# A linear-attention and expert kernel on Trainium2: five filling turnings become twelve small products, a decay table comes from two scans, and items 1 to 5 are ordered anew

## The chip, the cores and the metric

The kernel runs on one core of a Trainium2 chip. The metric is device time in microseconds (us), the median of several runs. The profile is one further execution, recorded by the hardware. A core has five engines that run their own instruction streams and wait for each other by semaphores: PE (TensorE, matrix products; each product is a weight load, shown as PEld, and a matmul), DVE (VectorE), ACT (ScalarE), POOL (GpSimd) and SP (SyncE, which here only issues DMAs).

## The reference

Two blocks follow each other. The first is a linear attention with a decay per channel (B=4 batches, H=8 heads, S=768 tokens, 48 channels per head), the second a layer of 8 experts (D=384, F=1024) with one expert per token; a gate lets a token keep the expert of the token before it.

```python
# attention, per batch and head
for t in range(S):
    kt, vt, rt = k[:, :, t], v[:, :, t], r[:, :, t]
    cur = einsum('bhd,bhe->bhde', u * kt, vt)
    y[:, :, t] = einsum('bhd,bhde->bhe', rt, state + cur)
    state = w * state + einsum('bhd,bhe->bhde', kt, vt)
x = y.transpose(0, 2, 1, 3).reshape(B, S, H * D_head)
# experts, per token
fresh_e = argmax(x @ w_gate)
e = fresh_e if s == 0 or sigmoid(x @ w_local) < 0.5 else prev_e
out[b, s] = softmax(x @ w_gate)[e] * (relu(x @ w1[e]) @ w2[e])
```

## The kernel before, in words

**Tiling.** The attention works on 16 items. Item n is one batch and one pair of heads (n // 4 and n % 4); a pair of heads lies on the partitions as two halves of 64. An item's 768 tokens are 6 chunks of 128. Within a chunk the sum over earlier tokens is a masked product of scores; across chunks the state is carried. Powers of the decay w, and their reciprocals, make both possible: rw is r times a power of w, kw is k times the reciprocal power.

**Steps of an item**, each with its method and the lines that the profile shows:

- load (L195 to L200): SP issues three transfers: rk, kv, vT. Up to four items are under way.
- scale (POOL): ke = k times the end powers (L214), pd = r times k (L218), rw (L235; items 0 to 2 have rw made by DVE in keys).
- keys (DVE): kw (L245), and for items 0 to 2 rw (L235).
- scores (L296, PE): 24 products in two halves, each into one of two PSUM banks called pair; DVE masks each half into am (L298).
- own (L275, PE): 4 products of pd with u, into the PSUM tile y; DVE multiplies y by vT (L281).
- added (L257, PE): 10 products of ke and v, the sums of each chunk, into a part of the PSUM tile mp.
- states (L263, DVE): one scan over these sums gives S, the state ahead of each chunk.
- inside (L305, PE): 12 products of am and v, added to y. before (L318, PE): 10 products of S and rw, added to y; ACT copies y out as xT (L326).
- turn (L337, PE): 6 transpositions of xT into a pair bank; ACT copies them to x (L339). logits (L349) and token_logits (L357) come once per batch and also use pair banks.

**Tables.** tab holds, for each of four head pairs, the powers 0 to 128 of w and of 1/w on each partition. They are made by doubling (L133): 7 multiplications, by DVE for pair 0 and by POOL for pairs 1 to 3. The powers of a pair are copied by ACT to first, a part of mp (L137, L383, L398). reciprocals refines the reciprocal powers in two steps on DVE (the newton steps, L157 and L158), from first into newton and inv. ends (ACT, L167 and L168) and turn_ends (PE, L174; ACT, L175) make the end powers, endT, on which ke depends; tables (ACT, L183) fills step, the factors of the scan S.

**What sets the order.** Every engine runs its instructions in the order in which they are issued, and that order is written out by hand in run (L363 on), with cases by item number; no scheduler changes it. Each call of banks takes the other one of the two pair banks, so a PE step that writes a pair bank waits until the reader of what stood there two calls ago is done. first, newton and the sums of added lie in the one tile mp. y has one buffer.

**Filling.** Ahead of item 0, PE has products that nothing uses: align(26) are 26 products of 32 by 32 by 128, warm(8) are 8 transpositions of 128 by 128, and, behind turn_ends for pair 0, warm(5) another 5.

Behind item 15 the expert stage follows: the router, hidden products, output products, gathers and scatters by DMA. It begins near 108 us and runs to the end.

Of the kernel before, what the change touches and what calls it, by code (L numbers as in the profile page):

```python
# [62 lines left out]
class Attention:  # L63
# [13 lines left out]
    def __init__(self, tc, st, rk_d, kv_d, vT_d, x_d, w_t, wp_d, kept, ident, lt, mp):  # L77
# [46 lines left out]
        w = once.tile([P, HP, 2], F32, name="w")  # L124
        nc.vector.tensor_scalar(w[:, :, 0], w_t[:, :, 0], W_LO, W_HI, Alu.max, Alu.min)
        nc.vector.reciprocal(w[:, :, 1], w[:, :, 0])
        nc.vector.tensor_copy(tab[:, 0, :, 1], w[:, 0])
        nc.gpsimd.tensor_copy(tab[:, 1:, :, 1], w[:, 1:])
        n = 2
        while n <= P:  # L130
            m = min(n - 1, P + 1 - n)
            for engine, t in ((nc.vector, tab[:, :1]), (nc.gpsimd, tab[:, 1:])):
                engine.tensor_mul(t[..., n:n + m], t[..., 1:1 + m], t[..., n - 1:n].to_broadcast([P, t.shape[1], 2, m]))  # L133
            n += m

        self.first, self.newton = mp[:, :P + 1], mp[:, P + 1:2 * P + 1]
# [6 lines left out]
        self.warm(8)  # L143
        self.ends(slice(0, 1))
        self.turn_ends(slice(0, 1))
        self.warm(5)

    def align(self, n):

# [211 lines left out]
    def run(self, router, fetch, heads):  # L361
# [11 lines left out]
        for n in range(M + 1):  # L373
            if n + AHEAD - 1 < M:
                self.load(n + AHEAD - 1)
            if n == 0:
                self.scale(0)
                self.keys(0)
                self.tables()
                self.scores(0, 0)()  # L380
                self.scores(0, 1)()
                self.own(0)
                self.nc.scalar.copy(self.first, self.tab[:, 1, 0])  # L383
                self.turn_ends(slice(1, HP))
                self.warm(3)
                self.added(0)
                self.reciprocals(1)
                self.states(0)
                self.scale(1)
                continue  # L390
            if n < 3:

                self.keys(n)
                self.inside(n - 1)
                self.before(n - 1)
                if n == 2:
                    self.turn(0, pair("tp"))
                self.nc.scalar.copy(self.first, self.tab[:, n + 1, 0])  # L398
                self.scores(n, 0)()
                keep = self.scores(n, 1)  # L400
                keep()
                self.own(n)
                self.added(n)
                self.states(n)
                if n == 1:
                    self.reciprocals(2)
                else:
                    router.numbering()
                self.scale(n + 1)
                continue  # L410
            if n < M:
                self.turn(n - 2, pair("tp"))
                if n == g + 7:
                    fetch(2)
                    router.head(self.inv[:, HP - 1])
                    heads()
                    self.own(n)
                if n == g + 6:
                    router.same(0, 1)
                if n == M - 2:  # L420
                    fetch(0)
                if n == 3:
                    self.reciprocals(3)
                if n < 5:
                    self.keys(n)
                if n > 3:
                    if n not in (g + 3, g + 5, g + 7):
                        self.added(n)
                    if n != g + 3:
                        self.states(n)  # L430
# [31 lines left out]
                continue  # L462

            ahead = n if n < 5 else n + 1
            if n == 3:
                self.added(3)
                self.states(3)
            if ahead < M:
                self.scores(ahead, 0)()
                if n == g + 6:  # L470
# [2 lines left out]
            if n % HP == 0:  # L473
# [7 lines left out]
                    router.ranks(0, (0,))  # L481
                self.logits(n // HP - 1, pair("lp")[0])
                if n == 4:
                    self.scores(5, 0)()
                    self.scores(5, 1)()
                    self.keys(6)
# [4 lines left out]
            else:  # L491
                if n == 3:
                    keep()
                self.own(n)
                if n == g + 2:
                    self.added(n + 1)
                    router.keys(0, mp)
# [1303 lines left out]
```

## Time and profile before

| what | value |
|---|---|
| time, median of 3 runs | 378.54 us (377.91 to 380.58) |
| the profiled execution's own time | 377.01 us |
| its span | 375.2 us |
| PE's mean granted clock | 0.997 of full speed |
| PE busy | 362.0 us (96%), 3844 instructions |
| PE weight loads | 318.4 us (85%) |
| DVE, POOL, ACT busy | 246.3, 152.1, 110.4 us |
| DMA | 74.93 MB, 200 GB/s in the mean |

In a row of the timeline stand the start in the span, the length, the engine, the line, the operation, out<-in, the size and the count (x24), and in brackets the idle time of the engine ahead of it with what ended it. Neighbouring instructions of a kind are one row; "issue" in brackets is a time in which the engine waited for nothing that the profile shows. The ends of matmuls are modelled. A group's row has the busy time and the mean of one in ns behind the first bar, and the idle time ahead of it behind the second.

### The profile page before, as it was taken

What the parts mean: (1) busy time and instruction counts of PE and PEld (TensorE: products, weight loads), DVE (VectorE), ACT (ScalarE), POOL (GpSimd) and SP (SyncE); (2) the same over time, 40 slices, a digit from 0 to 9 for tenths busy, and PEclk for the clock granted to TensorE, in tenths of its full rate; (3) what the DMA queues carried; (4) which work ended last, traced back from release to release, by engine and by line L of the source; (5) the groups of instructions that cost most, each with busy time, mean ns of one, the idle gap of its engine ahead of it and who ended that gap; (6) DMA issues with size and microseconds to landing.
All of it is one profiled execution on the core that took longest, in us unless ns stands there. A gap on an engine that the chain in (4) does not pass through costs nothing. (4 is left out here: it accounts for less than half of the span.)

```text
span 375.2 us, 9672 instructions
## 1 busy us (share of the span) xinstructions
PE 362.0 (96%) x3844; PEld 318.4 (85%) x3844; DVE 246.3 (66%) x717; ACT 110.4 (29%) x304; POOL 152.1 (41%) x212
## 2 busy tenths in 40 slices
PE   7899999999999999999999999999999999999992
PEld 6676777786769999989899999999998998989971
DVE  6988768788834845886567566857767767555300
ACT  4132232233432112322332233233233333331210
POOL 7689999789512055212433122313323023021012
PEclk9999999999999999999999999999999999999998
DMA  7999999983658749704342452264165064172011
GB/s 244 415 407 408 405 409 349 372 314 124 185 188 311 265 159 357 252 32 145 113 197 61 169 199 68 72 224 166 36 215 220 12 222 199 21 262 109 2 43 37
DMA packets 17765, 74.93 MB, mean 200 GB/s; under 512 B 2778, under 2 KB 6624, under 8 KB 15408
## 3 DMA queue, kind: packets, MB, share of 16 engines
q1 hardware_dynamic: 10336, 56.89, 41.1%
q0 software_dynamic: 3424, 9.48, 7.4%
q10 hardware_dynamic: 3952, 7.87, 5.7%
q8 instruction: 32, 0.52, 0.6%
q14 instruction: 21, 0.17, 0.1%
HBM read 64.79 MB, written 9.47 MB: 198 GB/s over the span
## 5 line engine op out<-in xcount | busy, mean ns | idle before, releaser
L1353 POOL DMA_INDIRECT out_dram<-yo,sid x27 | 26.6, 984 | 115.5 <-ACT yo L1348 92.0
L1204 PE MATMUL h<-exT,w1t 128*128 128x168 f32 (+4 forms) x240 | 54.9, 327 | 0.0
L1208 DVE TENSOR_TENSOR hT<-h,hs 128x168 f32<-128x168 f32 (+3 forms) x60 | 21.1, 351 | 46.2 <-PE h L1204 29.6
L1127 POOL DMA_INDIRECT xg<-x_d,gid x29 | 31.1, 1071 | 30.6 <-DVE gid L894 19.2
L1204 PEld LDWEIGHTS h<-exT,w1t 128*128 128x128 f32 x240 | 41.6, 190 | 0.3 <-issue 0.3
L1154 PE MATMUL h<-exT,w1t 128*128 128x168 f32 (+2 forms) x192 | 37.3, 332 | 0.0
L1273 PE MATMUL y<-factors,sums 128*128 128x192 f32 x168 | 36.8, 326 | 0.0
L298 DVE TENSOR_TENSOR am<-pair,kept 128x768 f32<-128x768 f32 x32 | 29.9, 952 | 9.7 <-PE pair L296 9.3
L1204 PE MATMUL h<-xs,ws 128*128 128x168 f32 (+4 forms) x144 | 35.3, 327 | 0.0
L218 POOL TENSOR_TENSOR pd<-rk 128x384 f32<-128x384 f32 x32 | 31.8, 1014 | 7.4 <-PE y L275 4.6
L1154 PEld LDWEIGHTS h<-exT,w1t 128*128 128x128 f32 x192 | 30.9, 190 | 2.0 <-issue 0.2
L1273 PEld LDWEIGHTS y<-factors,sums 128*128 128x128 f32 x168 | 28.9, 190 | 0.2
L1204 PEld LDWEIGHTS h<-xs,ws 128*128 128x128 f32 x144 | 25.5, 190 | 4.3 <-ACT hs L1211 1.2
L305 PE MATMUL y<-am,kv 128*64 128x128 f32 x360 | 22.8, 276 | 1.3 <-DVE y L281 1.2
L235 POOL TENSOR_TENSOR rw<-rk,tab 128x384 f32<-128x384 f32 x26 | 23.6, 931 | 0.4 <-DMA rk<-in_rk_dram 0.4
L296 PE MATMUL pair<-rw,kw 48*64 48x128 f32 (+1 forms) x768 | 22.8, 249 | 0.8 <-ACT end L168 0.6
L1273 PE MATMUL y<-w2t,hT 128*128 128x192 f32 x96 | 23.0, 328 | 0.0
L214 POOL TENSOR_TENSOR ke<-kv,endT 128x288 f32<-128x288 f32 (+1 forms) x32 | 21.9, 706 | 1.5 <-DMA kv<-in_kv_dram 1.5
L1141 DVE COPY exT<-tp 128x384 f32<-128x384 f32 (+5 forms) x29 | 13.8, 486 | 12.7 <-PE tp L1140 12.6
L296 PEld LDWEIGHTS pair<-rw,kw 48*64 48x64 f32 x768 | 19.4, 133 | 3.0 <-issue 1.1
L305 PEld LDWEIGHTS y<-am,kv 128*64 128x64 f32 x360 | 19.4, 137 | 3.0 <-DVE y L281 1.7
L326 ACT COPY xT<-y 128x768 f32<-128x768 f32 x15 | 12.0, 800 | 33.4 <-PE y L318 33.4
(305 smaller groups left out, 737.3 us busy)
## 6 DMA issues: line engine op xcount, KB each, us to landing
w1t<-in_w_dram SPq DMA_DIRECT2D x8, 1536.0 KB, 6.8
w2t<-in_w_dram SPq DMA_DIRECT2D x8, 1536.0 KB, 7.0
rk<-in_rk_dram SPq DMA_DIRECT2D x15, 768.0 KB, 10.4
kv<-in_kv_dram SPq DMA_DIRECT2D x16, 584.0 KB, 9.1
vT<-in_vT_dram SPq DMA_DIRECT2D x16, 384.0 KB, 8.1
x_d<-x ACTq DMA_DIRECT2D x4, 1152.0 KB, 8.0
w1t<-in_w_dram SPq DMA_DIRECT2D x2, 768.0 KB, 5.1
w2t<-in_w_dram SPq DMA_DIRECT2D x2, 768.0 KB, 4.5
```

The costliest lines, as they stand in the source:

```text
L214: nc.gpsimd.tensor_mul(t["ke"][:, z], t["k"][:, z], spread(self.endT[:, p, hp], 1, len(range(NCH)[z])))
L218: nc.gpsimd.tensor_mul(t["pd"][:, z], t["rT"][:, z], t["kT"][:, z])
L235: engine.tensor_mul(t["rw"][:, z], t["rT"][:, z], spread(pw, 1, z.stop - z.start))
L296: nc.tensor.matmul(sc[f * DP:(f + 1) * DP, h, i, x:], lhsT=t["kw"][q, c, o * DP:(o + 1) * DP], rhs=t["rw"][q, c, x:], start=True, stop=True)
L298: return lambda: nc.vector.tensor_mul(t["am"][:, g], sc, spread(self.kept[:, g:g + 3], 1, 2))
L305: nc.tensor.matmul(t["y"][h][p * DP:(p + 1) * DP, c2 * P:(c2 + 1) * P], lhsT=t["v"][:, (2 * c + h) * DH:(2 * c + h) * DH + DP], rhs=t["am" ...
L1127: self.nc.gpsimd.indirect_dma_start(out=xg[:n], out_offset=None, in_=self.x_d[:rows], in_offset=bass.IndirectOffsetOnAxis(ap=u["gid"][:n, ...
L1154: nc.tensor.matmul(h[:, :n], lhsT=u["w1"][:, m, kk, :], rhs=u["xT"][:, kk, :], start=(kk == 0), stop=(kk == DK - 1))
L1204: nc.tensor.matmul(out, lhsT=a, rhs=b, start=start and k == 0, stop=stop and k == len(terms) - 1, skip_group_check=True)
L1208: nc.vector.tensor_tensor(out, a, b, op=Alu.add)
L1273: return lambda: nc.tensor.matmul(bank[:, x * half:(x + 1) * half], lhsT=a, rhs=b, start=(j == 0 and x == 0), stop=(j == FK // 2 - 1), ski ...
L1353: self.nc.gpsimd.indirect_dma_start(out=out.rearrange("n (h d) -> (n h) d", h=2) if half else out, out_offset=bass.IndirectOffsetOnAxis(ap ...
```

## The change

1. Pair 0's powers come from two scans on DVE, one for w and one for 1/w, each over 128 elements with the running product times w (plus zero) as its step. They replace one copy and seven multiplications. POOL makes pairs 1 to 3 as before.
2. The 5 transpositions of warm(5) become 12 small products, align(12).
3. In item 0, the copy of pair 1's powers to first and the two newton steps for pair 1 are issued ahead of own(0).
4. turn(0) is issued in item 1, ahead of inside(1), where it stood behind before(1).
5. added and states of item 3 go behind own(3), where they stood ahead of the scores of item 4. Those of item 4 go behind the logits, ahead of the scores of item 5, where they stood ahead of inside(3). Those of item 5 go ahead of turn(3), where they stood behind it.

In the diff, the cases of run are by n, the number of the turn; in turn n PE does inside and before of item n - 1.

```diff
-        nc.vector.tensor_copy(tab[:, 0, :, 1], w[:, 0])
+        none = self.step[:, 0, 0, 0:1].to_broadcast([P, P])
+        for o in range(2):
+            nc.vector.tensor_tensor_scan(tab[:, 0, o, 1:], w[:, 0, o:o + 1].to_broadcast([P, P]), none, 1.0, Alu.mult, Alu.add)
         nc.gpsimd.tensor_copy(tab[:, 1:, :, 1], w[:, 1:])
-        n = 2
+        n, t = 2, tab[:, 1:]
         while n <= P:
             m = min(n - 1, P + 1 - n)
-            for engine, t in ((nc.vector, tab[:, :1]), (nc.gpsimd, tab[:, 1:])):
-                engine.tensor_mul(t[..., n:n + m], t[..., 1:1 + m], t[..., n - 1:n].to_broadcast([P, t.shape[1], 2, m]))
+            nc.gpsimd.tensor_mul(t[..., n:n + m], t[..., 1:1 + m], t[..., n - 1:n].to_broadcast([P, HP - 1, 2, m]))
             n += m
...
         self.turn_ends(slice(0, 1))
-        self.warm(5)
+        self.align(12)
...
                 self.scores(0, 1)()
+                self.nc.scalar.copy(self.first, self.tab[:, 1, 0])
+                self.reciprocals(1)
                 self.own(0)
-                self.nc.scalar.copy(self.first, self.tab[:, 1, 0])
                 self.turn_ends(slice(1, HP))
                 self.warm(3)
                 self.added(0)
-                self.reciprocals(1)
                 self.states(0)
...
                 self.before(n - 1)
-                if n == 2:
-                    self.turn(0, pair("tp"))
...
                 if n == 1:
+                    self.turn(0, pair("tp"))
                     self.reciprocals(2)
...
             if n < M:
+                if n == 5:
+                    self.added(5)
+                    self.states(5)
                 self.turn(n - 2, pair("tp"))
...
-                if n > 3:
+                if n > 5:
                     if n not in (g + 3, g + 5, g + 7):
                         self.added(n)
...
             ahead = n if n < 5 else n + 1
-            if n == 3:
-                self.added(3)
-                self.states(3)
...
                 self.logits(n // HP - 1, pair("lp")[0])
                 if n == 4:
+                    self.added(4)
+                    self.states(4)
                     self.scores(5, 0)()
...
                 self.own(n)
+                if n == 3:
+                    self.added(3)
+                    self.states(3)
```

The program's order on DVE, from its fourth instruction to the keys of item 0, before. w holds the decay and its reciprocal, tab the powers, mp holds first and newton.

```order
L125 TENSOR_SCALAR w<-w_t 128x4
L126 RECIPROCAL w<-w 128x4
L127 COPY tab<-w 128x2
L133 TENSOR_TENSOR tab<-tab 128x2
L133 TENSOR_TENSOR tab<-tab 128x2x2
L133 TENSOR_TENSOR tab<-tab 128x2x4
L133 TENSOR_TENSOR tab<-tab 128x2x8
L133 TENSOR_TENSOR tab<-tab 128x2x16
L133 TENSOR_TENSOR tab<-tab 128x2x32
L133 TENSOR_TENSOR tab<-tab 128x2x64
L157 SCALAR_TENSOR_TENSOR mp<-mp,tab 128x128
L158 SCALAR_TENSOR_TENSOR inv<-mp,tab 128x128
```

The same place after. The order writes a scan as SCALAR_TENSOR_TENSOR; the two of L129 are the new scans, and step stands for the zeros that they read.

```order
L125 TENSOR_SCALAR w<-w_t 128x4
L126 RECIPROCAL w<-w 128x4
L129 SCALAR_TENSOR_TENSOR tab<-w,step 128x128 x2
L158 SCALAR_TENSOR_TENSOR mp<-mp,tab 128x128
L159 SCALAR_TENSOR_TENSOR inv<-mp,tab 128x128
```

Eight instructions have become two; the newton steps behind them have kept their place. Lines behind this place have moved by one.

The program's order on PE at the start, before: the filling products (L152, L164), the turning of pair 0's end powers (L174), the scores of item 0 and its own.

```order
L152 MATMUL pair_149<-ident 32x32 x26
L164 MATMUL pair_148<-ident 128x128 x8
L174 MATMUL pair_149<-ident,end 128x128 x2
L164 MATMUL pair_148<-ident 128x128 x5
L296 MATMUL pair_149<-rw,kw 64x128 x12
L296 MATMUL pair_148<-rw,kw 64x128 x12
L275 MATMUL y<-pd,w_t 64x384 x4
```

The same place after.

```order
L153 MATMUL pair_149<-ident 32x32 x26
L165 MATMUL pair_148<-ident 128x128 x8
L175 MATMUL pair_149<-ident,end 128x128 x2
L153 MATMUL pair_148<-ident 32x32 x12
L297 MATMUL pair_149<-rw,kw 64x128 x12
L297 MATMUL pair_148<-rw,kw 64x128 x12
L276 MATMUL y<-pd,w_t 64x384 x4
```

The first three rows are the same but for their lines; behind them, 12 small products stand in the place of 5 turnings. A product of L152 shows as two matmuls and two weight loads in the trace (x52 for 26), a turning as one of each, so 5 pairs have become 24 and everything behind them on PE stands 19 pairs, or 38 instructions, later in the program.

The program's order on PE from item 5's scores to inside(4), before: the second half of the scores of item 5 (its last two rows), turn(3), added(5), token_logits(0), inside(4) and before(4). kv_162 is item 5's buffer, kv_166 item 4's.

```order
L296 MATMUL pair_148<-rw,kw 64x128 x2
L296 MATMUL pair_148<-rw,kw 64x64 x2
L337 MATMUL pair_149<-ident,xT 128x112 x6
L257 MATMUL mp<-kv_162,ke 48x48 x10
L357 MATMUL pair_148<-ident,lT 128x128 x3
L305 MATMUL y<-am,kv_166 64x128 x12
L318 MATMUL y<-rw,S 48x128 x10
```

The same place after.

```order
L297 MATMUL pair_148<-rw,kw 64x128 x2
L297 MATMUL pair_148<-rw,kw 64x64 x2
L258 MATMUL mp<-kv_162,ke 48x48 x10
L338 MATMUL pair_149<-ident,xT 128x112 x6
L358 MATMUL pair_148<-ident,lT 128x128 x3
L306 MATMUL y<-am,kv_166 64x128 x12
L319 MATMUL y<-rw,S 48x128 x10
```

added(5) and turn(3) have changed places.

The program's order on PE around own(4) and the logits, before: the logits stand directly ahead of the scores of item 5.

```order
L275 MATMUL y<-pd,w_t 64x384 x4
L349 MATMUL pair_148<-xT,wp 32x384 x8
L296 MATMUL pair_149<-rw,kw 64x128 x2
L296 MATMUL pair_149<-rw,kw 64x64 x2
L296 MATMUL pair_149<-rw,kw 64x128 x2
```

The same place after.

```order
L276 MATMUL y<-pd,w_t 64x384 x4
L350 MATMUL pair_148<-xT,wp 32x384 x8
L258 MATMUL mp<-kv_166,ke 48x48 x10
L297 MATMUL pair_149<-rw,kw 64x128 x2
L297 MATMUL pair_149<-rw,kw 64x64 x2
```

added(4) now stands between the logits and the scores of item 5. The orders of POOL and SP have not changed; on ACT the two copies of x of turn(0) now stand ahead of the copy of xT of item 1.

## The prediction, made before the changed kernel was run

> **What bounds the kernel now.** I read the page first, then the busy time by stage, then the timeline of the first 45 us with the waits of PE, because all that is changed stands before 45 us.
>
> The page, engine totals and the queue of instructions (packets, MB, share):
>
> ```profile
> PE 362.0 (96%) x3844; PEld 318.4 (85%) x3844; DVE 246.3 (66%) x717; ACT 110.4 (29%) x304; POOL 152.1 (41%) x212
> ...
> q8 instruction: 32, 0.52, 0.6%
> ```
>
> Busy time by stage (us, then PE, PEld, DVE, ACT, POOL, PE's granted clock, DMA share, GB/s):
>
> ```profile
> 20.00:40.43 20.43, 19.52 (x429) 14.22 (x428) 17.23 (x24) 5.77 (x13) 19.07 (x32) 1.00 1.02 409
> 40.43:108.00 67.57, 66.62 (x1440) 50.47 (x1439) 51.45 (x102) 22.06 (x57) 54.50 (x64) 1.00 0.80 297
> ```
>
> PE is the bound: from 40.43 us it is busy for 66.62 of 67.57 us, so what the first 40 us gain stays gained unless a transfer or POOL holds it back, and a stall of PE costs its full length. Before that POOL (19.07 of 20.43 us) and the DMA (share 1.02) are as full as PE, so a gain there has to be checked against both.
>
> **The start, DVE's table and PE's filling.** The timeline of the first 14 us:
>
> ```profile
> 1.55 2.96 PE L152 MATMUL pair<-ident 128*32 128x32 f32 x52 [1.55 <-POOL ident masks.py:199]
> ...
> 3.22 0.17 DVE L127 COPY tab<-w 128x2 f32<-128x2 f32 x1
> 3.42 1.87 DVE L133 TENSOR_TENSOR tab<-tab 128x2 f32<-128x2 f32 x7
> ...
> 4.45 1.09 PE L164 MATMUL pair<-ident 128*128 128x128 f32 x8
> ...
> 5.87 0.47 PE L174 MATMUL pair<-ident,end 128*128 128x128 f32 x2 [0.34 <-ACT end L167]
> ...
> 6.18 0.71 PE L164 MATMUL pair<-ident 128*128 128x128 f32 x5
> ...
> 7.46 1.72 PE L296 MATMUL pair<-rw,kw 48*64 48x128 f32 x48 [0.56 <-ACT end L168]
> ...
> 8.50 1.82 DVE L298 TENSOR_TENSOR am<-pair,kept 128x768 f32<-128x768 f32 x2 [0.26 <-ACT step L183]
> ...
> 10.24 0.96 DVE L281 TENSOR_TENSOR y<-y,vT 128x768 f32<-128x768 f32 x1
> ...
> 11.46 1.29 PEld L305 LDWEIGHTS y<-am,kv 128*64 128x64 f32 x24
> ...
> 11.82 0.30 DVE L157 SCALAR_TENSOR_TENSOR mp<-mp,tab 128x128 f32<-128x128 f32 x1 [0.63 <-PE mp L257]
> ...
> 12.36 0.64 DVE L263 TENSOR_TENSOR_SCAN S<-step,mp 128x240 f32<-128x240 f32 x1
> ...
> 13.06 0.68 PEld L318 LDWEIGHTS y<-rw,S 48*48 48x48 f32 x20 [0.30 <-DVE S L263]
> ...
> 14.03 0.57 PEld L296 LDWEIGHTS pair<-rw,kw 48*64 48x64 f32 x24 [0.29 <-issue]
> ```
>
> The table of pair 0 takes from 3.22 to 5.29 us. Two scans take its place. A scan over as many elements stands in the groups of DVE:
>
> ```profile
> L730 DVE TENSOR_TENSOR_SCAN run<-mp,seg 12x128 f32<-12x128 f32 x1 | 0.4, 400 | 0.0
> ```
>
> Two at 0.40 end at 4.02: 1.27 us less on DVE (with the S scan's 0.64 us per 240 elements, 0.34 for 128, it would be 1.4). Little of it arrives. PE still does its 26 and 8 filling products until 5.5 (4.45 + 1.09; the modelled ends may be 0.1 late, so I go by 5.4), then the two turnings, no longer held by end (0.31 from 5.87 to the next product at 6.18), and then the 12 new products, which are 24 pairs of weight load and matmul, since 26 products show as x52. At 2.96 us for 52 pairs they take 1.3 us, so the scores of item 0 begin at 7.05, not 7.46: 0.4 earlier. At the 0.53 us for 20 pairs that the sums of k and v take (row at 26.69, below) they take 0.55 to 0.65 and the scores begin at 6.4. I take 1.3, the row of the same form. Then y(0): the scores' masking (am, two of them in 1.82) moves from 8.50 to 8.05, but the two newton steps (2 x 0.30) now stand ahead of y(0), which goes from 10.24 to 10.47 and ends at 11.43. inside(0), which waits for y(0), starts 0.2 later, at 11.67, and ends at 12.96 (1.29). The newton steps no longer wait 0.63 for added(0), so S(0) follows y(0) at 11.4 instead of 12.36 and is done before 12.96: PE's 0.30 of waiting at 13.06 goes, and before(0) starts 0.1 earlier. DVE's kw(1) and rw(1) come 0.9 earlier with S(0), so the 0.29 at 14.03 goes too, which the profile puts to issue and I read as PE's wait for the first of them. 0.10 + 0.29 is 0.4 by the scores of item 1; **first term 0.35** (0 if the fill or kv of item 0 holds it, 0.6 at the short fill).
>
> **Items 1 to 5, the order on PE.** The timeline from 17 to 41 us:
>
> ```profile
> 17.72 1.29 PEld L305 LDWEIGHTS y<-am,kv 128*64 128x64 f32 x24 [0.94 <-DVE y L281]
> ...
> 20.01 0.58 PEld L337 LDWEIGHTS pair<-ident,xT 112*128 112x128 f32 x6
> ...
> 20.74 0.54 PEld L296 LDWEIGHTS pair<-rw,kw 48*64 48x64 f32 x24
> ...
> 21.59 1.89 DVE L298 TENSOR_TENSOR am<-pair,kept 128x768 f32<-128x768 f32 x2 [0.72 <-PE pair L296]
> ...
> 26.69 0.53 PEld L257 LDWEIGHTS mp<-kv,ke 128*48 128x48 f32 x20
> ...
> 27.19 1.35 POOL L214 TENSOR_TENSOR ke<-kv,endT 128x288 f32<-128x288 f32 x2 [0.96 <-DMA kv<-in_kv_dram]
> 27.28 1.08 PEld L296 LDWEIGHTS pair<-rw,kw 48*64 48x64 f32 x48
> ...
> 30.42 1.97 POOL L218 TENSOR_TENSOR pd<-rk 128x384 f32<-128x384 f32 x2
> ...
> 30.88 1.29 PEld L305 LDWEIGHTS y<-am,kv 128*64 128x64 f32 x24 [0.48 <-DVE y L281]
> ...
> 34.23 0.89 PE L275 MATMUL y<-pd,w_t 48*64 48x384 f32 x8
> ...
> 38.34 0.58 PEld L337 LDWEIGHTS pair<-ident,xT 112*128 112x128 f32 x6 [0.56 <-DVE am L298]
> 39.07 0.83 PEld L257 LDWEIGHTS mp<-kv,ke 128*48 128x48 f32 x20
> ...
> 40.43 1.29 PEld L305 LDWEIGHTS y<-am,kv 128*64 128x64 f32 x24 [0.17 <-issue]
> ```
>
> - turn(0) costs 0.73 us of PE (20.01 to 20.74), and DVE waits 0.72 us for the scores behind it (21.59). It moves ahead of inside(1), where PE waits 0.94 us for y(1). **0.73**; what is late next is DVE's rw(2), whose own 0.72 us of slack is just used up, so no less than 0.4. On ACT the two copies of x go ahead of the copy of xT(1), into a time in which ACT waits.
> - added(3) leaves the place ahead of the scores of item 3 (26.69 to 27.28): am, y(3) and inside(3) at 30.88 come **0.59** earlier. Behind own(3), where it now stands, PE waits for y(3) anyway. By here 0.35 + 0.73 + 0.59 = 1.67 us: own(4) would begin at 34.23 - 1.67 = 32.56. POOL has pd(4) ready at 30.42 + 1.97 = 32.39; it can't be earlier, since its chain hangs on kv landing at 27.19. So 1.84 is the most that this place lets through, and the forecast is just inside it.
> - added(4) stood in PE's wait for y(3) at no cost and now stands between the logits and the scores of item 5, with nothing to hide it: **-0.55** (0.53 plus a bubble; -0.4 to -0.65).
> - added(5) goes ahead of turn(3), into the 0.56 us in which PE waits for DVE's am to free the bank: **+0.56**. It now waits for S(4) (the sums' bank), which DVE does ahead of am(5); turn(3), inside(4) and all of item 4 are queued behind it. S(4) ends some 0.5 us before PE gets there, so I count nothing for the wait; if S(4) came late the 0.56 would go.
> - added(5) takes 0.83 us here, against 0.53 at 26.69: a stall of **0.30**, which is of the next kind.
>
> **PE's instruction blocks.** PE's weight loads, with the idle time ahead of them:
>
> ```profile
> 45.63 0.48 PEld L257 LDWEIGHTS mp<-kv,ke 128*48 128x48 f32 x17 [0.24 <-issue]
> ...
> 51.52 0.44 PEld L257 LDWEIGHTS mp<-kv,ke 128*48 128x48 f32 x16 [0.53 <-issue]
> ...
> 53.88 1.13 PEld L296 LDWEIGHTS pair<-rw,kw 48*64 48x64 f32 x46
> ...
> 55.14 0.21 PEld L275 LDWEIGHTS y<-pd,w_t 48*64 48x64 f32 x8
> ...
> 66.47 1.13 PEld L296 LDWEIGHTS pair<-rw,kw 48*64 48x64 f32 x46
> ...
> 67.74 0.21 PEld L275 LDWEIGHTS y<-pd,w_t 48*64 48x64 f32 x8
> ...
> 73.02 0.47 PEld L275 LDWEIGHTS y<-pd,w_t 48*64 48x64 f32 x8
> ```
>
> Within an even run of 20 loads PE stops for 0.24 and 0.53 us, waiting for nothing the profile shows. From one stop to the next lies one item: 10 + 12 + 10 + 24 + 4 products of two pairs and 6 turnings of one, 126 pairs or 252 instructions, and some waits. The instruction queue moved 0.52 MB in 32 packets, 16 KB each. So I read the stops as the crossing from one packet of about 256 instructions to the next, which comes at the same place of every item: in added of items 5, 6 and 7 (0.30, 0.24, 0.53), and in own of item 10, which took 0.47 instead of 0.21 us for eight loads (0.26). Counted on at that distance, the crossing near 67.7 falls on the end of the scores, and there it costs nothing: from the scores' last 46 loads to own it is 1.27 us at 66.47 and 1.26 at 53.88, where none falls. Five turnings (5 pairs) become 24 pairs, 38 instructions more, so each crossing falls 38 instructions earlier: out of added, across turn (12) and own (16), to the end of the scores for items 5 to 8, and into the middle of the scores for the later ones. **0.24 + 0.53 + 0.26 = 1.03** behind 40.43. Bounds: 1.3 if smaller stops go too, nothing if the end of the scores is missed by a few instructions and own pays 0.26 in each of four items.
>
> The Trainium skill, "Runtime: NRT & Kernel Launch", section "Instruction fetch mechanics", says that instructions come in blocks of 256 (16 KiB) and that crossing from one to the next is mostly hidden. The packets' size agrees; the stops of 0.24 and 0.53 us do not look hidden. By that rule the block terms are nothing and the sum would be 1.3 us shorter (first rival).
>
> **The sum.** 0.35 + 0.73 + 0.59 - 0.55 + 0.56 + 0.30 = 1.98 by 40.43, and 1.03 behind it: 3.0 us. Nothing else changes in POOL's and SP's order, and the expert stage after 108 us is the same. The profiled execution took 377.01 us (span 375.2), 1.53 below the median of 378.54: its successor would take 374.0, and the median 375.5.
>
> **The rivals.**
> 1. The stops are no crossings, or come back wherever the crossings fall. For it: the stops differ by a factor of two, and one crossing in added (56.67) hardly shows. Against it: their even distance. Gain 1.98 - 0.30 = 1.7, so 376.8.
> 2. The transfers and POOL hold the first 40 us: POOL starts ke(4) only when kv lands at 27.19, and from then on it is never idle until 55 us; with pd(4) or rw(4) a little later than I have it, own(4) and the scores of item 4 wait. For it: POOL 19.07 of 20.43 busy, DMA 1.02. Then only the blocks and some 0.5 us remain: gain 1.8 to 2.0 without the order's share, 376.6; with the blocks failing too, 378.
> 3. Slower: crossings cost more inside the scores than in added. With the largest stop seen (0.53) at each of the twelve crossings that now fall into scores (items 4 to 15), 6.4 us are added and 3.0 saved: 381.9. It decides from 0.25 us a crossing. Against it: the crossing at 67.7 cost nothing.
> 4. More than I have: the short fill and all small stops, 3.6 us, 374.9.
>
> **How the numbers follow.** Forecast (375.5, give or take 0.8) 0.55; rival 1 0.18; rival 2 0.15; rival 3 0.06; rival 4 0.06. About 1% (3.8 us) is what a measurement of this kernel can tell from no change, so faster means below 374.8 and slower above 382.3. The forecast lies 0.7 above the first line; the three runs before spread from 377.91 to 380.58, so a part of it, 0.13, and most of rival 4 fall below: faster 0.18. Only the outer half of rival 3 is above the second: slower 0.03. Same 0.79. The range takes in rival 4 with the runs' lower spread (374.9 - 0.6) and rivals 1 and 2 up to the blocks failing: 374.1 to 378.2.
>
> **What would show it.** Right: two scans near 0.40 on DVE and the scores of item 0 near 7.0; inside(1) with about 0.2 us of waiting instead of 0.94; turn(3) with no wait; inside(4) near 38.5 instead of 40.43; even runs of x20 in L258 (the new number of L257) of about 0.53 us, without a stop; the first product of the experts some 3 us earlier than now, and everything after it at that distance. Wrong: POOL waiting for DMA longer and own(4) for pd(4); stops inside the 46 loads of the scores or ahead of own; added(5) waiting for S(4); or an expert stage whose length is not the same.

## The result

The changed kernel is slower: 380.54 us in the median of 11 runs (379.35 to 383.5) against 378.63 us (377.31 to 381.2) of the kernel before on the same chips, a ratio of 1.0069 with a 95% interval of 1.0044 to 1.0093 (the two medians alone would give 1.0050). The forecast was 375.5, with a range up to 378.2. The profiled execution of the changed kernel took 382.31 us (span 380.6). It lies 1.8 above its median and that of the kernel before 1.6 below its own, so the two traces show 5.4 us of difference in span where the ratio stands for 2.6; what follows counts in the traces, and the experiments below weigh it.

The page of the changed kernel, PE's total and the instruction queue:

```profile
PE 362.7 (95%) x3863; PEld 319.2 (84%) x3863; DVE 245.1 (64%) x711; ACT 110.6 (29%) x304; POOL 152.4 (40%) x212
...
q8 instruction: 32, 0.52, 0.5%
```

PE does the 19 products more and is busy for 0.7 us more; the span is 5.4 us longer. So it is idle time that came. By stage (the same columns as before):

```profile
20.00:40.43 20.43, 17.39 (x404) 12.56 (x404) 15.10 (x22) 4.55 (x9) 18.98 (x32) 1.00 1.02 408
40.43:108.00 67.57, 65.12 (x1416) 49.85 (x1412) 53.01 (x103) 21.48 (x57) 54.97 (x64) 1.00 0.79 285
```

PE is busy for 17.39 of 20.43 us where it was busy for 19.52, and does 404 products in place of 429. The loss begins there.

The start went much as forecast, or better. The timeline of the changed kernel:

```profile
3.16 0.71 DVE L129 TENSOR_TENSOR_SCAN tab<-w,step 128x128 f32<-128x128 f32 x2
...
5.70 0.83 PEld L153 LDWEIGHTS pair<-ident 128*32 128x32 f32 x24 [0.17 <-issue]
...
6.58 1.30 PEld L297 LDWEIGHTS pair<-rw,kw 48*64 48x64 f32 x48
...
9.90 0.96 DVE L282 TENSOR_TENSOR y<-y,vT 128x768 f32<-128x768 f32 x1
...
12.64 0.56 DVE L246 TENSOR_TENSOR kw<-rk,inv 128x384 f32<-128x384 f32 x1 [0.49 <-DMA rk<-in_rk_dram]
...
13.78 1.41 PEld L297 LDWEIGHTS pair<-rw,kw 48*64 48x64 f32 x48 [0.39 <-issue]
...
17.64 1.29 PEld L306 LDWEIGHTS y<-am,kv 128*64 128x64 f32 x24 [0.48 <-DVE y L282]
...
19.91 0.82 PEld L297 LDWEIGHTS pair<-rw,kw 48*64 48x64 f32 x24
...
26.00 0.23 PEld L297 LDWEIGHTS pair<-rw,kw 48*64 48x64 f32 x7
```

The scores of item 0 start at 6.58 (before 7.46), those of item 1 at 13.78 (14.03), of item 2 at 19.91 (20.74), of item 3 at 26.00 (27.28). 1.28 us were gained by then, against 0.35 + 0.73 + 0.59 = 1.67 in the forecast.

Then the scores stop. PE's weight loads of the changed kernel, in one row each the end of a stop; the bracket is the idle time:

```profile
27.15 0.92 PEld L297 LDWEIGHTS pair<-rw,kw 48*64 48x64 f32 x41 [0.93 <-issue]
...
33.65 0.92 PEld L297 LDWEIGHTS pair<-rw,kw 48*64 48x64 f32 x41 [0.76 <-issue]
...
39.80 0.20 PEld L297 LDWEIGHTS pair<-rw,kw 48*64 48x64 f32 x7 [1.49 <-issue]
...
45.88 0.13 PEld L297 LDWEIGHTS pair<-rw,kw 48*64 48x64 f32 x1 [0.89 <-issue]
...
52.20 0.13 PEld L297 LDWEIGHTS pair<-rw,kw 48*64 48x64 f32 x1 [1.08 <-issue]
...
63.48 0.21 PEld L276 LDWEIGHTS y<-pd,w_t 48*64 48x64 f32 x8 [0.81 <-ACT xT L327]
```

The groups of the scores' loads, before and after (busy, mean in ns, then the idle time ahead of them and what the profile puts it to):

```profile
L296 PEld LDWEIGHTS pair<-rw,kw 48*64 48x64 f32 x768 | 19.4, 133 | 3.0 <-issue 1.1 <-ACT end L168 0.8 <-DVE rw L235 0.5
```

```profile
L297 PEld LDWEIGHTS pair<-rw,kw 48*64 48x64 f32 x768 | 20.5, 133 | 7.4 <-issue 6.6 <-ACT xT L327 0.2
```

Each stop comes after as many loads of an item's scores (of 48) as the count of 256 instructions gives: 7, 7, 41, 46, 47 and 48. The crossings are where the prediction put them. What it had wrong is what they cost: 0.93 + 0.76 + 1.49 + 0.89 + 1.08 + 0.81 = 5.96 us by 64 us, where the kernel before paid 0.30 + 0.24 + 0.53, and 0.26 in own of item 10. Three smaller stops follow at crossings in the scores of later items: 0.19, 0.56 and 0.32 at 75.76, 82.35 and 87.93. At inside(15) the changed kernel is 3.6 us late (107.65 against 104.06). Another 1.2 us come at the hand-over to the experts, where PE waits for the first gathered rows:

```profile
108.34 0.31 PEld L1140 LDWEIGHTS tp<-ident,xg 128*128 128x128 f32 x3 [1.20 <-DMA xg<-x_d,gid]
```

```profile
113.15 0.31 PEld L1145 LDWEIGHTS tp<-ident,xg 128*128 128x128 f32 x3 [2.43 <-DMA xg<-x_d,gid]
```

The first of the two rows is of the kernel before. In the profile of the first experiment, which has the same shift, this wait is 0.83 us, so these 1.2 us look like this one execution's own. From that product to the last group of the experts it is 257.25 us in place of 256.70.

### What the instruction queue shows

The trace has a record for each packet of the instruction queue, of 16384 bytes each for PE. I set them beside the times at which PE starts the first load of a new block (in the program's count of PE instructions, the 3rd, 4th ... block is entered behind instruction 706, 962, and so on by 256).

```
us                 3rd    4th    5th    6th    7th    8th    9th block
before   entered   21.6   27.3   33.3   39.5   45.6   51.5   56.8
         fetch of the next starts, after that entry:
                   24.71  30.95  37.04  43.23  49.20  54.57  59.44
         it ends   25.81  32.07  38.06  44.26  50.17  55.54  60.50
after    entered   20.3   27.15  33.65  39.80  45.88  52.20  57.25
         starts    24.71  31.07  37.31  43.50  49.73  54.44  61.23
         it ends   25.82  32.23  38.33  44.52  50.70  55.48  62.15
```

Two regularities hold in both. Where PE stops at a crossing, it goes on 1.3 to 1.5 us behind the end of that block's fetch: 27.15 - 25.82 = 1.33, 33.65 - 32.23 = 1.42, 39.80 - 38.33 = 1.47, 45.88 - 44.52 = 1.36, 52.20 - 50.70 = 1.50. And the fetch, which takes 0.9 to 1.2 us, starts only 3.0 to 4.5 us after PE has entered the block before it (2.2 and 2.6 in two cases behind 52 us). Where PE stops, it is 5.9 to 6.9 us from one entry to the next, and an item of 252 instructions needs about one block. So up to some 57 us a block takes longer to come than PE takes to work it off: without a stop between, an item takes 5.28 us (from inside(6) to inside(7) in the kernel before, 51.88 to 57.16).

This makes a theory, which the experiments call the supply theory: blocks arrive at times of their own, and whatever PE gains in between is taken back at the next crossing; an instruction added in front pushes work behind the next arrival. Its rivals are the order theory (the new places of added and turn cost the time) and the place theory (a crossing inside scores costs, one elsewhere not, which is the third rival of the prediction).

### The profile page after: what moved, and what is told of

It reads as the page before. It is cut to its first block, busy times and chain, and to the rows that moved or that the text cites. A ratio compares the mean times of both kernels' runs of the same rounds, so it can differ in the third digit from the quotient of the medians.

```text
span 380.6 us, 9705 instructions
## 1 busy us (share of the span) xinstructions
PE 362.7 (95%) x3863; PEld 319.2 (84%) x3863; DVE 245.1 (64%) x711; ACT 110.6 (29%) x304; POOL 152.4 (40%) x212
## 5 line engine op out<-in xcount | busy, mean ns | idle before, releaser
L297 PE MATMUL pair<-rw,kw 48*64 48x128 f32 (+1 forms) x768 | 25.0, 250 | 5.3 <-issue 5.0
L297 PEld LDWEIGHTS pair<-rw,kw 48*64 48x64 f32 x768 | 20.5, 133 | 7.4 <-issue 6.6
```

The lines of the kernel that those rows point to most:

```text
L297: nc.tensor.matmul(sc[f * DP:(f + 1) * DP, h, i, x:], lhsT=t["kw"][q, c, o * DP:(o + 1) * DP], rhs=t["rw"][q, c, x:], start=True, stop=True)
```

## The experiments

**The shift alone, and the order alone.** The kernel before with one line changed:

```diff
-        self.warm(5)
+        self.align(12)
```

> The kernel before with one edit: the five filling turnings become the twelve small products. Scans, newton steps and the order of items 1 to 5 stay as before. Supply theory: PE can enter its next block of 256 instructions only some 1.4 us after that block's fetch has ended, and the fetch starts late because data transfers fill the DMA engines, so two crossings lie at least 6.2 us apart until about 64 us. Moving every crossing 38 instructions forward makes PE arrive earlier at each: stops of 0.3 to 1.2 us at the crossings up to 64 us, 2 to 3 us slower in all, ratio 1.005 to 1.008, as slow as the changed kernel or slower. Order theory: the loss of the changed kernel comes from the new places of added and turn, so this kernel is as fast as the kernel before, ratio 0.999 to 1.001.

Measured: 380.84 us against 377.5, ratio 1.0074 (1.0046 to 1.0103). The one line alone costs as much as the whole change (1.0069). Weight loads of its profile:

```profile
39.66 0.20 PEld L296 LDWEIGHTS pair<-rw,kw 48*64 48x64 f32 x7 [1.47 <-issue]
...
46.05 0.13 PEld L296 LDWEIGHTS pair<-rw,kw 48*64 48x64 f32 x1 [1.11 <-issue]
...
52.09 0.13 PEld L296 LDWEIGHTS pair<-rw,kw 48*64 48x64 f32 x1 [0.85 <-issue]
```

The changed kernel with that line taken back:

```diff
-        self.align(12)
+        self.warm(5)
```

> The changed kernel with the five filling turnings back, so that the scans, the newton steps and the order of items 1 to 5 are new and the crossings fall where they fell in the kernel before. Supply theory: the 1.1 to 1.4 us that the order and the scans gain by 20 us show up, but from the crossing near 27 us on PE waits for the same fetches as before and the gain is lost again: ratio 0.998 to 1.002. Order theory: as slow as the changed kernel, ratio 1.005 to 1.009. My prediction's step on the order: 1.98 - 0.30 = 1.7 us faster, ratio 0.9955.

Measured: 377.63 us against 377.5, ratio 0.9992 (0.9964 to 1.0021). The order theory falls, and so does the 1.7 us that I gave the order. The weight loads show where its gain went:

```profile
25.89 0.53 PEld L297 LDWEIGHTS pair<-rw,kw 48*64 48x64 f32 x20
...
27.14 0.54 PEld L297 LDWEIGHTS pair<-rw,kw 48*64 48x64 f32 x23 [0.72 <-issue]
...
33.53 0.54 PEld L297 LDWEIGHTS pair<-rw,kw 48*64 48x64 f32 x22 [0.81 <-issue]
...
39.86 0.30 PEld L258 LDWEIGHTS mp<-kv,ke 128*48 128x48 f32 x9 [1.47 <-issue]
...
52.04 0.48 PEld L258 LDWEIGHTS mp<-kv,ke 128*48 128x48 f32 x17 [0.54 <-issue]
```

The scores of item 3 start at 25.89, 1.39 us earlier than before. The 4th block is entered at 27.14, the 5th at 33.53, the 6th at 39.86: 27.3, 33.3 and 39.5 before. The stops have taken back the gain.

**Another shift.** The changed kernel with 6 small products in place of 12:

```diff
-        self.align(12)
+        self.align(6)
```

> The changed kernel with 6 small products in place of 12, so every crossing falls 24 instructions later: for items 5 to 9 out of the end of the scores and to the start of turn or the logits, where PE's weight loads wait some 0.6 us anyway behind own's long products. Supply theory: the block's late arrival is partly hidden behind that 0.6 us and PE arrives later, so most of the loss goes: ratio 0.998 to 1.002. Place theory (a crossing inside scores costs 0.8 to 1.5 us whatever the fetch does, one in turn nothing): 3 us faster than the kernel before, ratio 0.991 to 0.994. Order theory: as slow as the changed kernel, 1.007.

Measured: 378.84 us against 377.5, ratio 1.0032 (1.0004 to 1.006): slower, a little outside what I expected of the supply theory, and far from the place theory's 0.991 to 0.994. In its profile the 4th to 6th blocks are entered at 26.7, 33.2 and 39.6 behind stops of 0.7 to 1.7 us, as in the others. The crossings of items 5 to 8 have no stop, but this is no clean reading: in this execution PE's granted clock was 0.50 from 39.8 to 43.2 us, so that PE came late to the first of them. With shifts of 0, 14 and 38 instructions, the new order gives 0.9992, 1.0032 and 1.0069.

38 instructions cost more than their share of a block (38/256 of 6.2 us is 0.9 us). The 9th block is entered at the same time, 57.3 to 57.4, with the order alone and with the shift alone; but PE then stands in added(8) in the first and at the end of the scores of item 8 in the second. Between the two lie own(7) and turn(6), which are 28 instructions but 1.5 us of PE (57.41 to 58.94 in the second). inside(7) starts at 57.73 and 59.43. So in these two executions the shift costs there what PE needs for the work that it pushes behind the crossing.

**What makes the fetch late.** Two kernels whose loads nearly stop after item 4; they leave out that part of the data, and the wrong values change what the experts do, so that only the attention stage is compared. The edit, in load:

```diff
-        if n:
+        if n > 4:
+            nc.sync.dma_start(out=rk[:, 0, 0], in_=self.rk_d[b, hp][:, :P])
+        elif n:
...
-        nc.sync.dma_start(out=kv, in_=self.kv_d[b, hp])
-        nc.sync.dma_start(out=vT.rearrange("p a c t -> p (a c t)"), in_=self.vT_d[b, hp])
+        if n < 5:
...
+        else:
+            nc.sync.dma_start(out=kv[:, :P], in_=self.kv_d[b, hp][:, :P])
+            nc.sync.dma_start(out=vT[:, 0, 0], in_=self.vT_d[b, hp][:, :P])
```

> The changed kernel, but items 5 to 15 load only the first 128 columns of rk and kv and one chunk of vT and work on what items 0 to 4 left in the buffers: that part of the computation is left out, the instructions and their order stay. After some 20 us the data transfers of the attention are nearly gone. If the fetch is late because data fill the DMA engines: it starts within 1.5 us of the crossing, no stop over 0.3 us stands inside scores behind 27 us, and the experts begin 5 to 8 us earlier than in the changed kernel. If the fetch takes its 6 us by itself: the stops of 0.8 to 1.5 us stay or grow, since PE gets there sooner.

> The kernel before with the light loads of the other run (items 5 to 15 load 128 columns of rk and kv and one chunk of vT and work on old data: that part of the computation is left out). Without data in the way the blocks come in time, so this shows what the order itself is worth: by my prediction's steps inside(4) starts 1.5 to 2 us later than in the changed kernel with light loads (39.63), and the experts 1.5 to 2 us later than 106.17. If the order is worth nothing or costs, the two are the same or the other way round.

The changed kernel with light loads, by stage and in its weight loads:

```profile
20.00:40.00 20.00, 18.83 (x423) 13.82 (x422) 16.46 (x24) 5.00 (x11) 18.52 (x25) 1.00 0.48 163
40.00:60.00 20.00, 20.00 (x484) 15.76 (x484) 15.66 (x37) 6.17 (x17) 20.00 (x25) 1.00 0.29 92
```

```profile
26.85 0.92 PEld L303 LDWEIGHTS pair<-rw,kw 48*64 48x64 f32 x41 [0.93 <-issue]
32.14 0.14 PEld L303 LDWEIGHTS pair<-rw,kw 48*64 48x64 f32 x2
32.24 1.13 PEld L303 LDWEIGHTS pair<-rw,kw 48*64 48x64 f32 x46
...
36.42 1.08 PEld L303 LDWEIGHTS pair<-rw,kw 48*64 48x64 f32 x48
...
41.62 1.13 PEld L303 LDWEIGHTS pair<-rw,kw 48*64 48x64 f32 x46
```

The stop at 26.85 is still there: its fetch started at 24.32, 4.3 us after the entry at 20.02, while the first items' data were flowing. Behind it the DMA share is 0.48 and then 0.29, the fetches start 1.25, 0.74, 0.68, 1.69, 0.49 and 0.19 us after their entries, and no stop is left, at the same crossings. The first product of the experts comes at 106.17, not 113.15 (waits for the data themselves are saved there too). In the kernel before with light loads the fetches behind the entries from 39 to 61 us start at most 0.2 us after them, five in a row, so the entry is what asks for the fetch, and the data in front of it are what makes it late. From entry to entry it would take some 3 to 4 us without them, an estimate from these starts, the fetch's own 0.9 to 1.4 us and the 1.4 us behind it. The first load of a block is only nearly the moment of asking: among the long products of the experts a fetch can start up to 2.6 us ahead of it (165.89 against 168.44 in the kernel before).

The kernel before with light loads has no stop at all, and the pair shows what the scans and the order are worth: inside(4) at 40.12 against 39.63, the first product of the experts at 106.39 against 106.17. That is 0.5 and 0.2 us, not the 1.5 to 2 that I expected. The stop of 0.93 stands in the changed kernel alone, so at inside(4) it would be some 1.4 without it, an estimate. From 40 to 60 us PE and POOL are both busy for 20.00 of 20.00 us in both kernels; whether 1.4 us would last to the experts is not shown. own(4), the scores of item 5 and inside(4), the changed kernel's two rows (its scores are above) and then the three of the kernel before:

```profile
33.58 0.24 PEld L282 LDWEIGHTS y<-pd,w_t 48*64 48x64 f32 x8 [0.20 <-POOL rw L242]
...
39.63 1.29 PEld L312 LDWEIGHTS y<-am,kv 128*64 128x64 f32 x24 [0.17 <-issue]
```

```profile
34.21 0.24 PEld L281 LDWEIGHTS y<-pd,w_t 48*64 48x64 f32 x8 [0.20 <-issue]
...
36.47 0.54 PEld L302 LDWEIGHTS pair<-rw,kw 48*64 48x64 f32 x24 [0.62 <-POOL ke L220]
...
40.12 1.29 PEld L311 LDWEIGHTS y<-am,kv 128*64 128x64 f32 x24 [0.17 <-issue]
```

The lead is 0.63 us at own(4), 0.05 at the scores of item 5 and 0.49 at inside(4).

**Fewer instructions in front.** If instructions in front cost, fewer should gain. The first filling made of 30 turnings (60 instructions in place of 120), in the new order (with warm(5)) and in the kernel before, and of 3 wide products with the 8 turnings in the new order (28 instructions, with warm(5)):

```diff
-        self.align(26)
-        self.warm(8)
+        self.warm(30)
```

> The order and the scans of the changed kernel, with the five filling turnings back and the first filling (26 small products and 8 turnings, 120 instructions) made by 30 turnings (60 instructions, about the same time on PE). All crossings fall 60 instructions later in the work than in the kernel before, 98 later than in the changed kernel. Supply theory: when the block near 27 us arrives, PE has 60 instructions more of the work behind it, which at 6.2 us for 256 is up to 1.45 us; the stops behind 27 us are shorter by that much in sum, and the order's gain can show: ratio 0.993 to 0.998 against the kernel before. Order theory: as the kernel with the new order alone (0.999) or slower.

> The kernel before, order and table included, with its first filling made by 30 turnings: the shift of 60 instructions alone. Supply theory: the kernel before had 1.2 us of stops by 52 us (0.11, 0.14, 0.24, 0.53 and 0.1 to 0.2 more at five crossings), so at most that is gained: ratio 0.996 to 0.999, and the run with the new order as well is faster than this one by 0.5 to 1.5 us. If the stops are no matter of the supply: 1.000.

```diff
+    def wide(self, n):
+        t = self.banks("warm")
+        for i in range(n):
+            self.nc.tensor.matmul(t[:, i % 2, :].rearrange("p (a b) -> p a b", a=4), lhsT=self.ident, rhs=spread(self.ident, 1, 4), start=True, stop=True)
...
-        self.align(26)
+        self.wide(3)
```

> As the run before, but the first 26 small products (104 instructions) become 3 products of 512 columns (12 instructions, some 2 to 4 us of PE) with the 8 turnings behind them: all crossings fall 92 instructions later than in the kernel before. Supply theory: up to 2.2 us of stops go, if PE's filling ends no later than before: ratio 0.991 to 0.997, not above the run with 60 instructions fewer. If the place of a crossing decides, and not how much work is behind it, this differs from that run in no fixed direction. Order theory: 0.999 or slower.

All three missed: 379.03 us (ratio 1.0047, 1.0023 to 1.007), 380.34 (1.0081, 1.005 to 1.0112) and 381.86 (1.0086, 1.0055 to 1.0117), each against 377.61. None is the shift alone, since the turnings took longer than I had reckoned: the scores of item 0 start at 7.52 in the first, against 7.12 with the new order alone, and at 7.79 in the second, against 7.42. The third is no clean test at all: the 3 products took 5.5 us and its scores start at 8.64. The first shows what I had overlooked. Block entries in us, 1st to 9th:

```
new order, shift 0    7.8  14.2  20.7  27.1  33.5  39.9  46.1  52.0  57.3
30 turnings           9.7  15.7  21.9  28.1  34.3  40.6  46.7  52.8  58.9
```

With fewer instructions in front, and 0.4 us more of filling, PE enters the first blocks later, each fetch is asked for at the entry before, and so the whole chain moves back by about 1 us, at 6.0 to 6.3 us a block. The arrivals are no fixed times; they hang on the entries. And with the crossings in own and inside the fetches start 3.6 us or more after them up to 62 us, where they came down to 2.0 to 2.6 behind 52 us in the kernel with shift 0. How much of that is the place is open.

**Slower work, same shift.** In scores, one product in the place of two for the even chunks, once with warm(5) and once with align(12), both in the new order:

```diff
+            if c % 2 == 0:
+                for h in range(2):
+                    q = slice(h * DP, h * DP + DH)
+                    nc.tensor.matmul(sc[:, h, i], lhsT=t["kw"][q, c], rhs=t["rw"][q, c], start=True, stop=True)
+                continue
```

> The order and the scans of the changed kernel, the five filling turnings back, and in scores one product of 64 by 128 by 128 in the place of two half products for the even chunks (masking removes what is computed too much): 12 products fewer of 48 pairs, 24 PE instructions of about 252 per item. Supply theory: a block comes every 6.1 to 6.3 us until about 60 us whatever PE does, so an item of 228 instructions takes 5.6 us there in place of 6.2; over items 2 to 8 that is 3.5 to 4 us, the crossing near 60 us comes after one item more of work, and later PE's own time is shorter by 6 pairs at some 0.03 us: ratio 0.985 to 0.992. If supply does not bind, only the pairs' own time goes: 12 x 0.027 = 0.3 us for an item while weight loads of 128 columns may take longer, 0.993 to 1.000, with the same stops as before.

> The changed kernel itself, twelve small products included, with the same merged scores. Supply theory: slower than the run with the five turnings by 38 instructions of supply, 0.9 us or less (the shorter items leave the supply behind earlier), ratio 0.987 to 0.995; stops stand at other places. Place theory (a crossing in scores costs, elsewhere not): the crossings now fall into inside, own and before, so the stops behind 40 us vanish and both runs are alike.

Measured: 390.34 us both, ratios 1.0303 (1.0251 to 1.0355) and 1.0309 (1.0256 to 1.0361) against 378.3. As a version it failed: in the first kernel's timeline four loads of the merged form (128 columns) take 0.30 us where eight of 64 columns take 0.21, and a whole item's scores take 2.1 us in place of 1.3:

```profile
52.62 0.30 PEld L295 LDWEIGHTS pair<-rw,kw 48*128 48x128 f32 x4
...
53.04 0.21 PEld L302 LDWEIGHTS pair<-rw,kw 48*64 48x64 f32 x8
...
53.41 0.30 PEld L295 LDWEIGHTS pair<-rw,kw 48*128 48x128 f32 x4 [0.16 <-issue]
...
54.74 0.29 PEld L276 LDWEIGHTS y<-pd,w_t 48*64 48x64 f32 x8
```

As a test it is clear. An item now takes 6.5 us for 228 instructions, so a block lasts 7 us or more (entries at 24.3, 31.3, 39.4, 46.6, 53.9, 61.2), the fetch ends 1.9 to 4.8 us ahead of the entry, and no stop stands at a crossing from there to 90 us, with the data flowing as before (DMA share 1.02 from 20 to 40 us). And there the shift of 38 instructions costs nothing that the runs show: 390.34 and 390.34. Against what I wrote for the second kernel, crossings do fall into scores: at 46.62, 53.90 and 61.19 in the first, and at six places from 23.19 to 82.64 in the second. The longest idle time at any of them is 0.12 us. So, with the changed kernel's crossings in scores under light loads, the place of a crossing has no price of its own; it costs where blocks are used up faster than they come.

**Smaller shifts the other way.** The first filling of 6 products and 25 turnings (74 instructions), and of 16 and 16 (96), in the new order with warm(5):

```diff
-        self.align(26)
-        self.warm(8)
+        self.align(6)
+        self.warm(25)
```

> The order and the scans of the changed kernel, the five filling turnings back, and the first filling made of 6 small products and 25 turnings: 74 instructions in place of 120 in about the same time (4.0 us by 0.115 and 0.136 us each), so crossings fall 46 instructions later in the work than in the kernel before, at the end of the scores or just behind them for items 0 to 4. Chain theory (each block is asked for at the crossing before, so the chain of crossings moves with the first ones, and what counts is the work done by a given crossing): the crossing near 20 us comes 0.3 to 0.5 us later than with the new order alone (20.74), as the scores' instructions pass at 14 ns each, and those behind it as much, while PE is 46 instructions or up to 1.1 us further on at each: ratio 0.995 to 0.999 if the delay of the fetch is as in that run, up to 1.003 if crossings in inside have longer delays (3.6 us, as with 60 instructions fewer, against 2.0 to 2.6).

> As the run before with 16 small products and 16 turnings first: 96 instructions in place of 120, crossings 24 instructions later than in the kernel before. By the chain theory about half of that run's effect while the stops bind: crossings near 20 us 0.2 us later, PE 24 instructions or up to 0.6 us further on: ratio 0.996 to 1.000. For items 4 and 8 to 11 the crossings fall into turn, where the fetch started after 1.8 to 2.6 us in the run with 6 small products: no stop over 0.3 us there.

Measured: 378.4 us (ratio 1.0023, 1.0001 to 1.0046) and 377.39 (0.9986, 0.996 to 1.0012) against 377.77. The first lies at the upper end of what was expected. The scores of item 0 start at 8.45 and 8.05, later than with the new order alone (7.12), so neither is the shift alone. In the first one's profiled execution one early fetch started 5.8 us after the entry (15.51 after 9.72), and PE stood for 2.04 us ahead of own(1), until 1.5 us behind the fetch's end. The profile names the pd that ends there, which by POOL's order is that of item 2 and not the one that own(1) reads:

```profile
18.07 0.33 PEld L276 LDWEIGHTS y<-pd,w_t 48*64 48x64 f32 x8 [2.04 <-POOL pd L219]
```

From 45 to 62 us its fetches start 0.4 to 1.4 us after the entries, and no stop is left there, although the DMA share is 0.95 from 40 to 50 us and 0.99 from 50 to 60. So the mean share does not say by itself how late a fetch starts; what does is open.

The second has the lowest ratio of all and is not told apart from the kernel before. Its profile has a stop of 1.04 within a turn, at 40.77, against my expectation that none over 0.3 would stand there. So no version was found that is clearly faster than the kernel before. In the new order, from 60 instructions fewer to 38 more in front, the ratios are 1.0047, 1.0023, 0.9986, 0.9992, 1.0032 and 1.0069; the first three also begin item 0 later by 0.4 to 1.3 us.

## Why the prediction was wrong

- **The start.** Right in kind: the scans take 0.71 us for two (0.80 expected), the twelve products 0.83 to 0.95 us, between my two prices of 0.65 and 1.3. The scores start at 6.58 where I had 7.05, but the first term came to 0.25 in place of 0.35 by the scores of item 1, since DVE waits 0.49 us for rk(1) to land.
- **turn(0) and added(3).** Right in the main: 0.58 (0.83 - 0.25) at the scores of item 2, of which 0.16 is lost again by inside(2) (23.73 against 24.40), and 0.59 where I had 0.73 and 0.59. 1.28 of 1.67 us were there at 26.00.
- **The rest of the order's sum** (added(4), added(5), and the bound by POOL at own(4)) can't be read in the changed kernel, since the stops stand between. With light loads it can: added(4) costs 0.58 us (0.63 - 0.05) where I had 0.55, and added(5) ahead of turn(3) gives 0.44 (0.49 - 0.05) where I had 0.56. So the order's terms were near the mark; with the data flowing the crossings take the gain back, and the order alone shows no gain in time (0.9992).
- **PE's instruction blocks**, the step that failed. I read the crossings rightly from the even distance of the stops and the packets of 16 KB, and placed them rightly. The failing step is the price: "Counted on at that distance, the crossing near 67.7 falls on the end of the scores, and there it costs nothing". It cost nothing because its block's fetch had ended 3.2 us before (64.59), not because of the place. I took each stop as the price of a crossing at a place, where it was the rest of a wait for a fetch that had a length of its own. So 1.03 + 0.30 us of gain became 5.96 us of stops by 64 us in the profile.
- **The third rival** had the sign and the point of decision right (crossings in scores, from 0.25 us each) and the price too low for the first six (0.53 taken, 0.76 to 1.49 measured), with 0.06 of the chances. Its reason, the place, is refuted by the light loads and by the merged scores, where crossings in scores cost nothing.
- **The second rival** saw that the DMAs, full at 1.02, would hold the first 40 us, through kv and POOL. They did, but through PE's instructions, which that rival does not name.
- **A crossing that is hidden.** The Trainium skill, "Runtime: NRT & Kernel Launch", section "Instruction fetch mechanics", says that a crossing is mostly hidden. Here that holds with light loads (no stop behind 27 us, at DMA shares of 0.48 and 0.29) and with merged scores (none from 24 to 90 us, at full DMA engines, with a block lasting 7 us or more). In the changed kernel, with a share of 1.02, the stops reach 1.49 us.
- **The size** of the loss, 2.6 us by the ratio, is that of the shift alone (1.0074). That the profiles show 3.6 at inside(15) is one execution against one.

## What to carry to other kernels

Where an engine issues short instructions while the DMA engines are full, look at the instruction queue's packets as at any other load: note when PE enters a block, when the next fetch starts and ends, and whether the block is used up before. Where it is, a gain of order between two crossings can be taken back at the next one, and instructions added or left out far ahead move every later crossing: here 38 more cost 0.7%, and leaving some out did not reliably gain. A stop's length at one place says nothing of another place, until it is known what the stop was waiting for.

## What was not expected of the hardware

- PE goes on 1.2 to 1.6 us behind the end of the fetch that it waited for, at every stop at a crossing over 0.3 us in the profiles here.
- The fetch, one packet of 16 KB of about 1.0 us, starts between 0.0 us (the kernel before with light loads) and 5.8 us after the entry that precedes it, mostly 3.0 to 4.5 us from 20 to 50 us with a DMA share of about 1.02.
- Up to 360 us PE's granted clock fell to 0.50 at four places in the profiles of whole kernels, for 3.4 to 6.8 us: around stops of 1.66 us (align(6) in place of align(12), from 39.8), 2.04 us (74 instructions in front, from 17.7) and 2.08 us (the wide products, from 65.0), and behind a wait of 2.34 us at 101.22 in the last. After stops of 1.49 us and less it stayed at 1.00, but it did so too after the changed kernel's wait of 2.43 us at 113.15. That a long stop brings it is not shown.
- The 11 runs of the changed kernel spread by 4.2 us (379.35 to 383.5), those of the two kernels with merged scores, which have no stops, by 0.6 and 1.1 (6 runs each). That the fetches' delay makes the spread is a guess.
